# The last two chunks of an attention and feed-forward kernel: the product with w_out by seven block products in place of eight

## The chip, the cores and the metric

The kernel runs on one core of one Trainium2 chip. Five engines work beside each other, each with its own queue of instructions: TensorE (PE in the profile; its weight loads are PEld) multiplies matrices into PSUM, VectorE (DVE) and ScalarE (ACT) work elementwise, GpSimd (POOL) hardly computes here, and SyncE (SP) issues the DMA transfers. The metric is the device time of one execution in microseconds (us). Three executions of the kernel before took 653.5, 653.57 and 654.96 us; the median is 653.57.

## The reference

Eight batches of eight heads, 512 token rows and 32 state rows a head, 64 numbers a row. Tokens attend to the states and states to the tokens; the heads are put side by side, and a two-layer network follows, whose activation is h - tanh(h):

```
scores  = x @ state.T / 8;  a  = softmax(scores);   xread = a @ state
scores2 = state @ x.T / 8;  a2 = softmax(scores2);  sread = a2 @ x
y = concat([xread, sread], rows)       # (8 batches * 544 rows, 512)
h = y @ w_in                           # 512 -> 2048
out = (h - tanh(h)) @ w_out            # 2048 -> 512
```

All of it is float32. h - tanh(h) is an odd function: a row of y with its sign turned gives a row of the output with its sign turned.

## The kernel before

The rows are handled in nine **chunks**. Chunks 0 to 7 are the 512 token rows of a batch each; chunk 8 is the 256 state rows of all batches. For a token chunk the read of the states and w_in are folded into one matrix m (256 rows per half, made once per batch by `m_units` and `m_first_two` and kept in DRAM as `mdram`), so that the hidden layer of a token chunk is the product of the attention weights `aT` with m; that of chunk 8 is the state reads `srT` times w_in.

A chunk has 16 **steps**, one per block of 128 of the 2048 hidden columns. In a step, `hidden(f)` (lines 406 to 421) computes h for that block; `finish` takes tanh on ACT and the difference on DVE (line 426). Then `split` (lines 119 to 122) cuts the result into two parts: ACT rounds it to the faster matmul format (the high part), and DVE subtracts that from the original (the low part). Weights are cut the same way. A product of two such pairs takes three matmuls: high by high, high by low, low by high. `output(f)` (lines 431 to 460) multiplies the 128 hidden columns by 128 rows of w_out for each block of 128 tokens, three matmuls of 512 columns (lines 458 to 460), and adds up in PSUM over the 16 steps: four PSUM banks for a token chunk, two for chunk 8. After the last step the banks are copied to SBUF and stored.

Per step, a token chunk thus issues 6 hidden and 12 output matmuls of 512 columns; chunk 8 issues 12 hidden matmuls of 256 columns and 6 output matmuls of 512. Over a chunk of 512 tokens the product with w_out is 192 matmuls, over chunk 8 it is 96. `wo[f]` keeps both parts of w_out in SBUF, 16 tiles of 2 x 512 columns.

**Order.** The steps of all chunks stand in one list (line 849; 144 steps). In the loop (lines 851 to 894) the hidden step two places ahead (LAG = 2) is put before the output step, so hidden and output matmuls alternate on TensorE and a step's tanh, difference and cut have two steps' time. The other work (attention of later batches, the m of later batches) is hung on steps by the table `SCH` (line 163): a number in a list is the step at which one unit of that work is issued. Each unit is kept, on ACT and DVE, behind the tanh of its step (`issue_after`). Within these rules a planner orders the instructions of each queue by its own estimate of when each is ready; a matmul can so be put ahead of an earlier one whose operand it expects later. The first steps, up to step 8, follow an order written out by hand (lines 798 to 814).

**Loads.** SP issues every transfer. m of a chunk is loaded per quarter q (`load_m`, lines 229 to 250); batches 6 and 7 have their m in two addends, added on DVE (line 247). Chunk 8 loads w_in by quarters (`load_win`, lines 252 to 268). The state reads are turned for chunk 8 by eight PE transposes (`turn_sread`, lines 381 to 389).

## Time and profile before

| | |
|---|---|
| median of three runs | 653.57 us |
| the profiled execution | 653.85 us |
| its span, first to last instruction | 652.1 us |
| granted TensorE clock | 1.000 |
| PE busy | 646.6 us (99%), 3892 matmuls |
| DVE busy | 445.5 us (68%), 795 instructions |
| ACT busy | 355.6 us (55%), 645 instructions |
| POOL busy | 1.2 us, 7 instructions |
| DMA | 95.89 MB, all data on one queue (SP's) |

The span is 1.75 us shorter than the profiled execution's own time, which lies 0.28 us above the median. PE counts as busy while any matmul is in flight; since matmuls overlap, the busy share says that it never rests, and not how fast it goes: for that one reads the distance between the starts of two matmuls. In a row of the profile the operation stands as output <- inputs, with partitions x elements, count, total and mean time, and at the end the idle time of the engine before it and what ended it.

### The profile page before, as it was taken

The page shows a single profiled execution, that of the slowest core. Times are in us where ns is not written, and L with a number is a line of the kernel's source. Part 1 is how long each engine was busy: PE and PEld are TensorE (multiplying, and loading weights), DVE is VectorE, ACT ScalarE, POOL GpSimd, SP SyncE. Part 2 cuts the span into 40 slices and gives each one's busy share as a digit, 9 for nine tenths or more (in the row PEclk, how much of TensorE's full clock was granted, in tenths as well). Part 3 has the DMA queues.
Part 4 walks back from the last instruction along what each step waited for, and adds up shares of the span by engine and source line. Part 5 has one row for each costly group of instructions (what it writes and reads, how often), then busy time and mean ns, then how long its engine had stood idle before and what let it go on. Part 6 is the DMA issues. An engine that isn't in the chain of part 4 may idle for free.

```text
span 652.1 us, 10247 instructions
## 1 busy us (share of the span) xinstructions
PE 646.6 (99%) x3892; PEld 511.1 (78%) x3892; DVE 445.5 (68%) x795; ACT 355.6 (55%) x645; POOL 1.2 (0%) x7
## 2 busy tenths in 40 slices
PE   9999999999999999999999999999999999999997
PEld 6466766888877788887888788887887888888996
DVE  5998999898556676558765875458767654454442
ACT  4865668786665545546556655444534453333442
POOL 0000000000000000000000000000000000000000
PEclk9999999999999999999999999999999999999999
DMA  9994787267577512444366227353342202010310
GB/s 314 380 311 159 258 270 266 61 197 223 143 250 210 165 33 100 128 130 152 111 195 186 80 94 224 104 184 139 123 136 96 66 33 98 0 33 32 130 34 32
DMA packets 52209, 95.89 MB, mean 147 GB/s; under 512 B 6208, under 2 KB 21568, under 8 KB 52160
## 3 DMA queue, kind: packets, MB, share of 16 engines
q1 hardware_dynamic: 52160, 95.24, 45.3%
q8 instruction: 30, 0.49, 0.3%
q14 instruction: 19, 0.16, 0.1%
HBM read 64.29 MB, written 30.93 MB: 146 GB/s over the span
## 4 chain that ended last, share of the span: by engine, by line
PE 96%; DVE 1%; ACT 1%; DMA 0%; issue 0%; POOL 0%; ACTq 0%; POOLq 0%
PE ops L458 19%; PE ops L460 19%; PE ops L459 19%; PE hps L418 9%; PE hps L419 9%; PE hps L420 9%; PE hps L729 3%; PE mps L219 2%; PE mps L673 1%; PE rps L368 1%; PE ops L755 1%; PE pps L355 1%; PE mps L218 1%; PE sps L283 1%; PE warm L582 1%; PE hps L416 1%
## 5 line engine op out<-in xcount | busy, mean ns | idle before, releaser
L458 PE MATMUL ops<-wo,g 128*128 128x512 f32 x536 | 214.1, 401 | 0.1
L459 PE MATMUL ops<-wo,g 128*128 128x512 f32 x536 | 209.0, 390 | 0.0
L460 PE MATMUL ops<-wo,g 128*128 128x512 f32 x536 | 198.2, 391 | 0.0
L426 DVE TENSOR_TENSOR t<-hps,t 128x512 f32<-128x512 f32 (+1 forms) x134 | 87.7, 656 | 95.6 <-ACT t L426 94.8
L426 ACT ACTIVATE t<-hps 128x512 f32<-128x512 f32 (+1 forms) x134 | 76.3, 573 | 125.7 <-PE hps L420 124.3
L458 PEld LDWEIGHTS ops<-wo,g 128*128 128x128 f32 x536 | 100.6, 188 | 25.8 <-issue 2.5
L460 PEld LDWEIGHTS ops<-wo,g 128*128 128x128 f32 x536 | 100.2, 188 | 22.7 <-DVE g L122 0.8
L459 PEld LDWEIGHTS ops<-wo,g 128*128 128x128 f32 x536 | 100.7, 188 | 22.0 <-issue 2.2
L121 ACT CAST g<-t 128x512 fp32r<-128x512 f32 (+1 forms) x134 | 79.6, 596 | 61.7 <-DVE t L426 56.8
L122 DVE TENSOR_TENSOR g<-t,g 128x512 fp32r<-128x512 f32 (+1 forms) x134 | 87.4, 655 | 31.4 <-ACT g L121 29.6
L419 PE MATMUL hps<-aT,m 128*128 128x512 f32 x232 | 90.7, 391 | 0.0
L418 PE MATMUL hps<-aT,m 128*128 128x512 f32 x232 | 90.7, 392 | 0.0
L420 PE MATMUL hps<-aT,m 128*128 128x512 f32 x232 | 90.1, 391 | 0.0
L418 PEld LDWEIGHTS hps<-aT,m 128*128 128x128 f32 x232 | 43.5, 188 | 11.8 <-DVE t L426 1.3
L420 PEld LDWEIGHTS hps<-aT,m 128*128 128x128 f32 x232 | 43.6, 188 | 10.6 <-issue 1.7
L419 PEld LDWEIGHTS hps<-aT,m 128*128 128x128 f32 x232 | 43.6, 188 | 9.6 <-issue 0.8
L122 DVE TENSOR_TENSOR m<-mr,m 128x1024 fp32r<-128x1024 f32 x29 | 35.4, 1221 | 14.2 <-ACT m L121 13.7
L122 DVE TENSOR_TENSOR wst<-w,wst 64x512 fp32r<-64x512 f32 (+1 forms) x56 | 36.3, 648 | 6.1 <-ACT wst L121 4.5
L121 ACT CAST m<-mr 128x1024 fp32r<-128x1024 f32 x29 | 30.3, 1045 | 10.3 <-DMA mr<-md 10.2
L220 ACT COPY st<-mps 128x512 f32<-128x512 f32 (+1 forms) x56 | 30.2, 557 | 10.1 <-PE mps L219 9.1
L121 ACT CAST wst<-w 64x512 fp32r<-64x512 f32 (+1 forms) x56 | 32.9, 587 | 0.8
L481 DVE COPY ob<-ops 128x512 f32<-128x512 f32 x14 | 9.7, 690 | 16.4 <-DMA out_x<-ob 10.9
(219 smaller groups left out, 626.9 us busy)
## 6 DMA issues: line engine op xcount, KB each, us to landing
md<-st SPq DMA_DIRECT2D x96, 128.0 KB, 2.2
mr<-md SPq DMA_DIRECT2D x20, 512.0 KB, 3.7
xT<-in_xT SPq DMA_DIRECT2D x16, 512.0 KB, 5.5
xn<-in_xn SPq DMA_DIRECT2D x16, 512.0 KB, 4.2
out_x<-ob SPq DMA_DIRECT2D x32, 256.0 KB, 2.5
w<-wf SPq DMA_DIRECT2D x12, 512.0 KB, 4.3
wn<-wf SPq DMA_DIRECT2D x8, 512.0 KB, 4.0
ml<-md SPq DMA_DIRECT2D x6, 512.0 KB, 3.8
```

What stands on the lines that cost most here:

```text
L121: nc.scalar.copy(hi, src)
L122: return (sub or nc.vector).tensor_sub(lo, src, hi)
L219: nc.tensor.matmul(ps, s[:, 0, h], t[:, e], start=(g == 1), stop=True)
L220: nc.scalar.copy(stage[:, e], ps)
L418: nc.tensor.matmul(ps, mhi[k][:, cols], ahi[:, k], start=(k == 0), stop=False)
L419: nc.tensor.matmul(ps, mhi[k][:, cols], alo[:, k], start=False, stop=False)
L420: nc.tensor.matmul(ps, mlo[k][:, cols], ahi[:, k], start=False, stop=(k == nk - 1))
L426: tanhs.append((nc.scalar.activation(t, ps, AF.Tanh).ins, nc.vector.tensor_sub(t, ps, t).ins))
L458: nc.tensor.matmul(o, g[:, 0, tok], wo[f][:, 0], start=first, stop=False)
L459: nc.tensor.matmul(o, g[:, 0, tok], wo[f][:, 1], start=False, stop=False)
L460: return nc.tensor.matmul(o, g[:, 1, tok], wo[f][:, 0], start=False, stop=last).ins
L729: nc.tensor.matmul(hps[n], m[:, k], ats[b][k], start=(k == 0), stop=(k == 1))
```

## The change

For chunks 7 and 8 a new class `Seven` replaces `Chunk`. Each group of 256 tokens (two in chunk 7, one in chunk 8) is treated as a product of 2 x 2 blocks: the hidden values are blocks A of 128 tokens by 1024 hidden columns (even and odd blocks of 128), w_out is blocks B of 1024 by 256. Eight block products would be needed; Strassen's scheme in Winograd's form needs seven, with sums of blocks before and after:

```
S1 = A21+A22  S2 = S1-A11  S3 = A11-A21  S4 = A12-S2
P1 = A11 B11      P2 = A12 B21      P3 = S4 B22      P4 = A22 (B11-B12-B21+B22)
P5 = S1 (B12-B11) P6 = S2 (B22-B12+B11)  P7 = S3 (B22-B12)
```

The four results are sums of the seven. The parts of the change:

- **The products.** `finish` writes h - tanh(h) into a buffer `big` that holds all blocks; nothing is multiplied by w_out until the hidden steps are done. `operand` then cuts one block (128 x 1024) into high and low parts, three products ahead of its use (AHEAD = 3). `products` issues, for each of 8 depth steps, one matmul of the high part with 512 columns (the two parts of a 256-column weight block side by side) and one of the low part with 256; in P3 of chunk 8 three matmuls of 256. So a product is 16 matmuls, and a group of 256 tokens 112. `gather` adds the two halves of the bank and sums the products on ACT and DVE; `store` writes results of 128 x 256.
- **Sums of blocks of A.** S1 and S2 on DVE. S3 and S4 by accumulating DMAs from POOL's queue in chunk 7, by DVE in chunk 8. So that only additions are needed in chunk 7, half of batch 7's rows get their sign turned in the softmax sums (`signs`).
- **Sums of blocks of w_out** (`weight_sums`), in eight parts of three stages each, hung on steps 41 to 105 by the new list "sums": stage one puts the whole weights together again (two loads on SP, two accumulating DMAs on POOL's queue), stage two forms the four sums (three ACT instructions, four accumulating DMAs, of which three follow each other), stage three cuts them into parts (ACT 128 x 1024, DVE 128 x 1024) and stores both to DRAM (`tdram`). `fetch` loads a sum's parts for a product, eight transfers of 256 KB each on SP: those of P4 and P6 over a quarter of `wo`, those of P5 and P7 into tiles of their own.
- **Order.** In chunks 7 and 8 the loop of steps ends; hidden steps come first (even ones now in PSUM's `ps_o` banks), then the products in the order P4 P1 P5 P2 P6 P7 P3, for chunk 7 each for both groups. Loads and cuts of m and w_in for these chunks are issued earlier than before. m's second addend of batch 7 is added by an accumulating DMA and not by DVE. `SCH` has new numbers; the last attention unit of batch 7 moves from step 121 to 114.
- **Buffers.** Several tiles of earlier stages (raw w_in and w_out rows, kept scores, m of batch 1) now lie in slices of `big`.

The diff without the new numbers of `SCH` and the moves into `big`:

```diff
+AHEAD = 3
+FIRST = 7
...
+        return cut_m(b, q, raw_m(b, q))
+
+    def raw_m(b, q):
...
-            r = pool.tile([P, 2, 512], F32, tag="mr", name=f"mr{b}{q}", bufs=RRB)
+            tag, bufs = ("stage", SB) if b >= FIRST else ("mr", RRB)
+            r = pool.tile([P, 2, 512], F32, tag=tag, name=f"mr{b}{q}", bufs=bufs)
...
-            if len(addends) > 1:
+            if len(addends) > 1 and b >= FIRST:
+                nc.gpsimd.dma_start(r, addends[1].rearrange("g h n f -> (h n) g f"), accum_op=ALU.add)
+            elif len(addends) > 1:
                 r2 = pool.tile([P, 2, 512], F32, tag="stage", name=f"ml{b}{q}", bufs=SB)
...
+            if b < FIRST:
+                nc.vector.tensor_scalar_add(z, z, EPS)
+            else:
+                nc.vector.scalar_tensor_tensor(z, z, EPS, signs, ALU.add, ALU.mult)
...
+    blocks = big.rearrange("p f n -> p (f n)").rearrange("p (g r c k n) -> p g r c k n", g=2, r=2, c=2, n=P)
+
+    def weight_sums(p):
+        r = parts(f"wr{p}", [P, 2, 512], F32)
+        for c in range(2):
+            w = wo[2 * p + c].bitcast(F32)
+            nc.sync.dma_start(r[:, c], w[:, 0])
+            nc.gpsimd.dma_start(r[:, c], w[:, 1], accum_op=ALU.add)
+        yield
+        x = r.rearrange("p k (c n) -> p k c n", c=2)
+        t = parts(f"wt{p}", [P, 4, 256], F32)
+        nc.scalar.activation(t[:, 0::2], x[:, 0], AF.Copy, scale=-1.0)
+        nc.scalar.copy(t[:, 1], x[:, 0, 0])
+        nc.scalar.activation(t[:, 3], x[:, 1, 0], AF.Copy, scale=-1.0)
+        for to, add in ((t[:, 0], x[:, 0, 1]), (t[:, 2], x[:, 1, 1]), (t[:, 1], t[:, 2]), (t[:, 3], t[:, 1])):
+            nc.gpsimd.dma_start(to, add, accum_op=ALU.add)
+        yield
+        hi, lo = parts(f"wh{p}", [P, 4, 256], F32R), parts(f"wl{p}", [P, 4, 256], F32R)
+        split(hi, lo, t)
+        for c, part in enumerate((hi, lo)):
+            nc.sync.dma_start(tdram[:, :, p, 256 * c : 256 * c + 256], part.bitcast(F32))
+        yield
+
+    class Seven(Chunk):
+        ORDER = "P4 P1 P5 P2 P6 P7 P3".split()
+        banks = {}
+        seconds = []
+
+        def finish(self, f, ps):
+            n = self.n
+            t = blocks[:, : n // 256, :, f % 2, f // 2]
+            ps = ps.rearrange("p (g r n) -> p g r n", r=2, n=P)
+            nc.scalar.activation(t, ps, AF.Tanh)
+            Seven.gate = nc.vector.tensor_sub(t, ps, t).ins
+
+        def block(self, g, name):
+            return blocks[:, g, int(name[0]) - 1, int(name[1]) - 1]
+
+        def side(self, g, name):
+            a11, a12, a21, a22 = (self.block(g, x) for x in ("11", "12", "21", "22"))
+            out, a, b = {"S1": (a22, a21, a22), "S3": (a21, a11, a21), "S2": (a22, a22, a11), "S4": (a12, a12, a22)}[name]
+            if self.i == B:
+                (nc.vector.tensor_add if name == "S1" else nc.vector.tensor_sub)(out, a, b)
+            elif name in ("S1", "S2"):
+                nc.vector.tensor_add(out, a, b)
+            else:
+                nc.gpsimd.dma_start(out, b if out is a else a, accum_op=ALU.add)
+
+        HOME = {"P4": "22", "P1": "11", "P5": "22", "P2": "12", "P6": "22", "P7": "21", "P3": "12"}
+
+        def operand(self, x, g, ks):
+            if (x, g) not in self.parts:
+                self.parts[x, g] = (
+                    pool.tile([P, NFF // 2, P], F32R, tag="g", name=f"hi{self.i}{x}{g}", bufs=GB),
+                    parts(f"lo{self.i}{x}{g}", [P, NFF // 2, P], F32R),
+                )
+            hi, lo = self.parts[x, g]
+            with tc.issue_after(self.gate):
+                Seven.gate = split(hi[:, ks], lo[:, ks], self.block(g, self.HOME[x])[:, ks]).ins
+
+        def weights(self, x, k):
+            if x in ("P1", "P2", "P3"):
+                f, c = {"P1": (0, 0), "P2": (1, 0), "P3": (1, 1)}[x]
+                return wo[2 * k + f][:, :, 256 * c : 256 * c + 256]
+            if x in ("P4", "P6"):
+                return wo[2 * k][:, :, 256:512]
+            return Seven.seconds[k]
+
+        def fetch(self, x):
+            row = {"P5": 0, "P6": 1, "P7": 2, "P4": 3}[x]
+            if not Seven.seconds:
+                for k in range(4):
+                    tag, bufs = ("t", TB) if k < 3 else ("cr", CB)
+                    Seven.seconds.append(pool.tile([P, 2, 256], F32R, tag=tag, name=f"second{k}", bufs=bufs))
+                last = pool.tile([P, 4, 2, 256], F32R, tag="sm", name="second", bufs=1)
+                Seven.seconds.extend(last[:, k] for k in range(4))
+            for k in range(NFF // 2):
+                nc.sync.dma_start(
+                    self.weights(x, k).bitcast(F32), tdram[:, row, k].rearrange("p (c n) -> p c n", c=2)
+                )
+
+        def products(self, x, g, ks):
+            if (x, g) not in self.banks:
+                self.banks[x, g] = bank(ps_o, f"{x}{self.i}{g}")
+            o = self.banks[x, g]
+            hi, lo = self.parts[x, g]
+            last = NFF // 2 - 1
+            for k in ks:
+                w = self.weights(x, k)
+                if self.i == B and x == "P3":
+                    nc.tensor.matmul(o[:, :256], hi[:, k], w[:, 0], start=(k == 0), stop=False)
+                    nc.tensor.matmul(o[:, :256], hi[:, k], w[:, 1], start=False, stop=False)
+                    nc.tensor.matmul(o[:, :256], lo[:, k], w[:, 0], start=False, stop=(k == last))
+                    continue
+                both = lambda: nc.tensor.matmul(o.rearrange("p (c n) -> p c n", c=2), hi[:, k], w, start=(k == 0), stop=(k == last))
+                if k < last:
+                    both()
+                nc.tensor.matmul(o[:, :256], lo[:, k], w[:, 0], start=False, stop=False)
+                if k == last:
+                    both()
+
+        def gather(self, x, g):
+            o = self.banks.pop((x, g))
+            if g not in self.sums:
+                self.sums[g] = twins(f"c{self.i}{g}", [P, 4, 256], F32)
+            u = [self.sums[g][:, k] for k in range(4)]
+            if x == "P3" and self.i == B:
+                nc.vector.tensor_add(u[2], u[1], o[:, :256])
+                self.store(g, 0, 1, u[2])
+                return
+            p = u[{"P4": 3, "P1": 0, "P5": 1, "P2": 2, "P6": 0, "P7": 2, "P3": 2}[x]]
+            add, sub = nc.vector.tensor_add, nc.vector.tensor_sub
+            if self.i < B and x in ("P1", "P2", "P7", "P3"):
+                nc.scalar.activation(p, o[:, 256:], AF.Copy, scale=-1.0)
+                sub(p, p, o[:, :256])
+            else:
+                nc.scalar.copy(p, o[:, 256:])
+                add(p, p, o[:, :256])
+            if x == "P1":
+                sub(u[3], u[0], u[3])
+            elif x == "P5":
+                add(u[1], u[1], u[0])
+            elif x == "P2":
+                add(u[2], u[2], u[0])
+                self.store(g, 0, 0, u[2])
+            elif x == "P6":
+                add(u[1], u[1], u[0])
+                add(u[3], u[3], u[0])
+            elif x == "P7":
+                add(u[3], u[3], u[2])
+                self.store(g, 1, 0, u[3])
+                add(u[0], u[1], u[2])
+                self.store(g, 1, 1, u[0])
+            elif x == "P3":
+                add(u[2], u[1], u[2])
+                self.store(g, 0, 1, u[2])
+
+        def store(self, g, r, c, u):
+            t = 2 * g + r
+            nc.sync.dma_start((xout[self.i] if self.i < B else sout)[t * P : (t + 1) * P, 256 * c : 256 * c + 256], u)
+
+        def hidden_bank(self, f):
+            return ps_h if f % 2 else ps_o
+
+        def units(self, start=0):
+
+            i, gs = self.i, range(self.n // 256)
+            self.parts, self.sums, self.banks = {}, {}, {}
+            seq = [(x, g) for x in self.ORDER for g in gs]
+            each = 1.37 if i < B else 1.44
+            made = 2
+            for f in range(start, NFF):
+                if f == start:
+                    self.fetch("P4")
+                    self.fetch("P5")
+                self.hidden(f)
+                if f in (3, 7):
+                    self.cut(f // 4 + 2)
+                if f % 4 == 1 and f > 4:
+                    self.open(slice(f // 2 - 2, f // 2), seq[:made])
+                yield each
+            self.open(slice(6, 8), seq[:made])
+
+            def make(n):
+                if made <= n < len(seq):
+                    x, g = seq[n]
+                    self.operand(x, g, slice(0, 8))
+                    if x == "P5":
+                        self.side(g, "S2")
+                        self.side(g, "S3")
+                    elif x == "P2":
+                        self.side(g, "S4")
+
+            for n in range(made, AHEAD):
+                make(n)
+            for n, (x, g) in enumerate(seq):
+                for ks in ((range(6), range(6, 8)) if n == 0 else (range(8),)):
+                    self.products(x, g, ks)
+                make(n + AHEAD)
+                self.gather(x, g)
+                if g == gs[-1]:
+                    if x == "P4":
+                        self.fetch("P6")
+                    elif x == "P5":
+                        self.fetch("P7")
+                if i < B:
+                    if n == 2:
+                        chunks[i + 1].raw(0)
+                        if i + 1 < B:
+                            chunks[i + 1].raw(1)
+                    elif n in (5, 9):
+                        chunks[i + 1].cut(n // 9)
+                    elif n == 8 and i + 1 == B:
+                        with tc.issue_after(self.gate):
+                            turn_sread()
+                yield 2.77
+
+        raws = None
+
+        def raw(self, q):
+            self.raws = self.raws or {}
+            with tc.issue_after(self.gate):
+                self.raws[q] = raw_m(self.i, q) if self.i < B else raw_win(q)
+
+        def cut(self, q):
+            with tc.issue_after(self.gate):
+                self.m[q] = (cut_m if self.i < B else cut_win)(*((self.i,) if self.i < B else ()), q, self.raws[q])
+            q += 2 if self.i < B else 1
+            if q < 4:
+                self.raw(q)
+
+        def prepare(self, q):
+            pass
+
+        def open(self, ks, operands):
+            for x, g in operands:
+                self.operand(x, g, ks)
+                if x == "P4" and ks.stop == 8:
+                    self.side(g, "S1")
...
-    chunks = [Chunk(i) for i in range(B + 1)]
+    chunks = [(Chunk if i < FIRST else Seven)(i) for i in range(B + 1)]
...
+    sums = itertools.chain(*[weight_sums(p) for p in range(NFF // 2)])
+    end = HALF + NFF + HALF + NFF * (FIRST - 2)
+
+    def side_work(st):
+        advance(sums, SCH["sums"].count(st))
...
+    for st, (i, f) in list(enumerate(steps))[HALF:end]:
...
+        if st >= end - 7:
+            Seven.gate = tanhs[st][-1]
+            if st == end - 5:
+                chunks[FIRST].raw(0)
+                chunks[FIRST].raw(1)
+            elif st == end - 4:
+                chunks[FIRST].cut(0)
+            elif st == end - 2:
+                chunks[FIRST].cut(1)
...
+    st, passed = end, 0.0
+    for i in range(FIRST, B + 1):
+        for spent in chunks[i].units(LAG if i == FIRST else 0):
+            passed += spent
+            while passed > 3.79:
+                passed -= 3.79
+                with tc.issue_after(chunks[i].gate):
+                    side_work(st)
+                st += 1
```

More of the change, by code (lines that the diff above doesn't have):

```diff
@@ L204, in m_units @@
             for k in range(2):
-                w = pool.tile([P, 2, 512], F32, tag="wf", name=f"w1{g}{q}{k}", bufs=WB)[:, :, cols]
+                w = home(10 + 2 * (next(wfn) % 2), 2)[:, :, cols]
                 nc.sync.dma_start(w, wf[q][:, 2 * k : 2 * k + 2, cols])
@@ L250, in load_m, with raw_win, cut_win @@
         return [m[:, 0, k] for k in range(2)], [m[:, 1, k] for k in range(2)]
-    def load_win(q):
-        his, los = [], []
-        for k in range(2):
-            w = pool.tile([P, 2, 512], F32, tag="wf", name=f"wn{q}{k}", bufs=WB)
-            nc.sync.dma_start(w, wf[q][:, 2 * k : 2 * k + 2])
-            if k == 0:
-                m = pool.tile([P, 2, 2, 512], F32R, tag="m", name=f"wm{q}", bufs=MB)
-                split(m[:, 0], m[:, 1], w)
-                his += [m[:, 0, c] for c in range(2)]
-                los += [m[:, 1, c] for c in range(2)]
-            else:
-                for c in range(2):
-                    m = parts(f"wm{q}{c}", [P, 2, 512], F32R)
-                    split(m[:, 0], m[:, 1], w[:, c])
-                    his.append(m[:, 0])
-                    los.append(m[:, 1])
+    def raw_win(q):
+        raws = []
+        for k in range(2):
+            w = pool.tile([P, 2, 512], F32, tag="stage", name=f"wn{q}{k}", bufs=SB)
+            nc.sync.dma_start(w, wf[q][:, 2 * k : 2 * k + 2])
+            raws.append(w)
+        return raws
+    def cut_win(q, raws):
+        his, los = [], []
+        for k, w in enumerate(raws):
+            if k == 1 and q % 2:
+                halves = [pool.tile([P, 2, 512], F32R, tag="x", name=f"wm{q}{c}", bufs=XB) for c in range(2)]
+                for c in range(2):
+                    split(halves[c][:, 0], halves[c][:, 1], w[:, c])
+                    his.append(halves[c][:, 0])
+                    los.append(halves[c][:, 1])
+                continue
+            tag, bufs = ("aT", 1) if k else ("m", MB)
+            m = pool.tile([P, 2, 2, 512], F32R, tag=tag, name=f"wm{q}{k}", bufs=bufs)
+            split(m[:, 0], m[:, 1], w)
+            his += [m[:, 0, c] for c in range(2)]
+            los += [m[:, 1, c] for c in range(2)]
         return his, los
     def convert_wout(f, part):
-        w = pool.tile([P, 512], F32, tag="wor", name=f"wor{f}", bufs=RB)
+        w = big[:, 14 + f % 2]
         part.convert(w)
@@ L516, in convert_win @@
         if p % 2 == 0:
-            wfs[q, p // 2] = pool.tile([P, 2, 512], F32, tag=("wf", "stage")[q - 2], name=f"w0{q}{p // 2}", bufs=WB)
+            if q == 2:
+                wfs[q, p // 2] = home(10 + 2 * (next(wfn) % 2), 2)
+            else:
+                wfs[q, p // 2] = pool.tile([P, 2, 512], F32, tag="stage", name=f"w0{q}{p // 2}", bufs=SB)
         w0[q][p].convert(wfs[q, p // 2][:, p % 2])
@@ L625, in turn_back @@
         if j < 2:
[L626 removed]
+            ats[0][j] = big[:, 4 + j]
         else:
@@ L850, in attention_ffn @@
     steps += [(i, f) for i in range(2, B + 1) for f in range(NFF)]
-    for st, (i, f) in list(enumerate(steps))[HALF:]:
+    sums = itertools.chain(*[weight_sums(p) for p in range(NFF // 2)])
+    end = HALF + NFF + HALF + NFF * (FIRST - 2)
+    def side_work(st):
+        advance(sums, SCH["sums"].count(st))
+        advance(a0, SCH["a0"].count(st))
+        advance(second_split, SCH["at1"].count(st))
+        advance(first_split, SCH["at0"].count(st))
+        advance(late1, SCH["r1"].count(st))
+        for b in range(2, B):
+            n = SCH[f"att{b}"].count(st)
+            if n:
+                if b not in atts:
+                    atts[b] = new_attention(b)
+                advance(atts[b], n)
+        for g in range(2):
+            advance(m1[g], SCH[f"m{g}"].count(st))
+    for st, (i, f) in list(enumerate(steps))[HALF:end]:
         with ExitStack() as gates:
```

52 lines of the change are left out of this document (24 added, 28 removed).

## The prediction

> **What bounds the kernel now.** I read the page's busy times first, then its chain of waits, then busy time by stretch.
>
> ```profile
> span 652.1 us, 10247 instructions
> ...
> PE 646.6 (99%) x3892; PEld 511.1 (78%) x3892; DVE 445.5 (68%) x795; ACT 355.6 (55%) x645; POOL 1.2 (0%) x7
> ...
> PE 96%; DVE 1%; ACT 1%; DMA 0%; issue 0%; POOL 0%; ACTq 0%; POOLq 0%
> ```
>
> ```profile
> 200.00:330.00 130.00, 130.00 (x842) 105.12 (x841) 88.16 (x166) 70.74 (x125) 0.00 (x0) 1.00 0.42 130
> 330.00:470.00 140.00, 140.00 (x787) 113.49 (x789) 93.77 (x174) 75.28 (x132) 0.00 (x0) 1.00 0.46 144
> 537.00:608.00 71.00, 71.00 (x394) 59.42 (x393) 34.29 (x54) 26.30 (x45) 0.00 (x0) 1.00 0.15 52
> 608.00:652.00 44.00, 40.34 (x251) 36.02 (x249) 17.04 (x36) 16.26 (x38) 0.00 (x0) 0.99 0.15 50
> ```
>
> (A row: stretch, length, then PE, PEld, DVE, ACT, POOL busy, granted clock, DMA share, GB/s.) TensorE sets the time: never idle between 200 and 648 us, clock 1.00, 96% of the chain. DVE is busy 67% of the middle and 48% of the stretch in which chunks 7 and 8 run. So a matmul removed is time gained, as long as the other engines keep up. The price of a matmul is its distance to the next, not its 0.39 us duration. The timeline of TensorE in chunk 7 and in chunk 8:
>
> ```profile
> 569.79 0.39 PE L459 MATMUL ops<-wo,g 128*128 128x512 f32 x1
> ...
> 574.10 0.39 PE L460 MATMUL ops<-wo,g 128*128 128x512 f32 x1
> ...
> 608.80 0.28 PE L418 MATMUL hps<-srT,wm 128*128 128x256 f32 x1
> ...
> 610.24 0.40 PE L458 MATMUL ops<-wo,g 128*128 128x512 f32 x1
> ...
> 611.62 0.28 PE L418 MATMUL hps<-srT,wm 128*128 128x256 f32 x1
> ```
>
> Chunk 7: 20 rows, 4.31 us in 19 steps, 0.2268 us per 512-column matmul. Chunk 8: twelve 256-column matmuls in 1.44 us, 0.120 each; six of 512 columns in 1.38 us, 0.230 each. So the cost is 13.3 ns plus 0.417 ns per column, and weight loads of 0.19 us each don't slow even the short ones.
>
> **TensorE's share of the change.** Per 256 tokens the output product was 96 matmuls of 512 columns. Now it is 7 products of 8 steps, a step being one matmul of 512 columns (high part against both weight halves) and one of 256: 8 x (0.2268 + 0.120) = 2.774 us. Chunk 7 (two groups): 192 x 0.2268 = 43.55 becomes 14 x 2.774 = 38.84, saving 4.71. Chunk 8: 96 x 0.230 = 22.08 becomes 6 x 2.774 + 24 x 0.120 (its P3 has three short matmuls a step) = 19.52, saving 2.56. Should the long matmul cost 0.230 beside short ones, 0.5 us goes. The hidden products keep their counts. **TensorE: -7.3 us, bounds -6.8 and -7.3.**
>
> That counts columns, though the instructions rise from 96 to 112 per group. The Trainium skill ("TensorE: Matmul & The Clock Gate", Back-to-back issue gap) gives streams with weight loads about 81 ns at 128 columns and 131 ns at 512, nearly a fixed price per instruction. By it, 256 columns taken in between at an estimated 98 ns, 112 x 114.5 = 12.8 us would replace 96 x 131 = 12.6. The trace disagrees with 227 and 120 ns.
>
> **What the other engines must now deliver.** Hidden and output matmuls no longer alternate: 16 hidden steps, then the products, each of which needs an operand of 128 x 1024 cut in two by ACT and DVE, and sums. Durations by shape:
>
> ```profile
> L122 DVE TENSOR_TENSOR m<-mr,m 128x1024 fp32r<-128x1024 f32 x29 | 35.4, 1221 | 14.2 <-ACT m L121 13.7 <-DMA md<-st 0.2
> L121 ACT CAST m<-mr 128x1024 fp32r<-128x1024 f32 x29 | 30.3, 1045 | 10.3 <-DMA mr<-md 10.2
> L121 ACT CAST g<-t 128x512 fp32r<-128x512 f32 x118 | 73.1, 622 | 52.3 <-DVE t L426 47.4 <-PE ops L460 3.2 <-PE mps L673 0.9
> L426 DVE TENSOR_TENSOR t<-hps,t 128x512 f32<-128x512 f32 x118 | 80.9, 688 | 84.0 <-ACT t L426 83.3
> L426 ACT ACTIVATE t<-hps 128x512 f32<-128x512 f32 x118 | 70.2, 599 | 113.9 <-PE hps L420 112.5 <-PE hps L416 0.9
> L122 DVE TENSOR_TENSOR g<-t,g 128x256 fp32r<-128x256 f32 x16 | 6.8, 424 | 6.1 <-ACT g L121 5.2 <-PE ops L460 0.9
> L121 ACT CAST g<-t 128x256 fp32r<-128x256 f32 x16 | 6.5, 406 | 9.5 <-DVE t L426 9.4
> L426 ACT ACTIVATE t<-hps 128x256 f32<-128x256 f32 x16 | 6.1, 383 | 11.8 <-PE hps L420 11.8
> L122 DVE TENSOR_TENSOR g<-t,g 128x512 fp32r<-128x512 f32 x118 | 80.6, 687 | 25.2 <-ACT g L121 24.4
> L386 PE MATMUL tps<-ident,sr x8: 270/272/273, 596.8 to 597.5; 128*128 128x128 f32 x8
> ```
>
> Hidden stage, chunk 7: 6 x 0.2268 = 1.36 us a step against 0.60 of ACT and 0.69 of DVE; the m and first-operand cuts fit the remainder. Chunk 8: 1.44 against 0.38 and 0.42.
>
> DVE while chunk 7's products run: 12 whole operands at 1.22 (14.6), last slices of two (0.85), S1 and S2 twice (4.9), 30 sums of 256 columns at 0.42 (12.6), the next chunk's w_in cuts 3 x 1.22 + 2 x 0.69 (5.0), the turned state reads 2 x 0.69 (1.4), the last tanh difference 0.7: 40.1 us, of which some 2.9 (the last three products' sums) may come later, so 37.2 against TensorE's 38.8 + 0.9 of transposes. Chunk 8: 5 whole operands 6.1 + slices 0.85 + S1 to S4 4.9 + 14 sums 5.9 + 0.4 = 18.2 against 19.5. ACT has about 25 us in chunk 7. So DVE goes from half busy to about 93% and must not wait much.
>
> In strict program order that costs: after chunk 7's last hidden matmul 0.60 + 0.69 + 0.41 + 0.42 and four handoffs of 0.06 (an estimate; successors start 0.03 to 0.10 after) make 2.4 us plus some delay, the six ready steps cover 2.08: about 0.5 lost. P4's second group waits behind S1 (1.22) and its own slice: 1.0. In chunk 8 P1 waits the same way: 0.85; P2 and P6 behind S2, S3, S4: 0.35. Together 2.7. But TensorE's queue is written by a planner that moves ready matmuls ahead of late ones:
>
> ```profile
> 600.84 0.39 PE L458 MATMUL ops<-wo,g 128*128 128x512 f32 x1
> 601.07 0.39 PE L459 MATMUL ops<-wo,g 128*128 128x512 f32 x1
> 601.29 0.39 PE L458 MATMUL ops<-wo,g 128*128 128x512 f32 x1
> ...
> 601.98 0.84 PE L460 MATMUL ops<-wo,g 128*128 128x512 f32 x3
> ```
>
> Here the low-part matmuls (L460), whose operand was late, were held back without a gap. The six ready steps of the next product can fill such holes. Bounds 0 and 2.7; I take 1.4, the middle.
>
> **Weight sums, steps 41 to 105.** Eight times 0.62 + 2 x 0.41 + 1.05 us of ACT (19.9) and 1.22 of DVE (9.8, less three adds of m that go, 3 x 1.22: 6.1), over 64 steps or more than 260 us in which a third of DVE and 45% of ACT is free. They add 32 DMAs on SP's queue and 48 accumulating ones on POOL's, which the trace has none of. What waits for those: stage three's cast, which stops everything behind it on ACT, the next tanh above all, and so TensorE. Stage two's last three accumulations follow each other; stage three comes four steps (4 x 18 x 0.2268 = 16.3 us) later. Nearest rows:
>
> ```profile
> q1 hardware_dynamic: 52160, 95.24, 45.3%
> md<-st SPq DMA_DIRECT2D x96, 128.0 KB, 2.2
> mlast<-f SPq DMA_DIRECT2D x8, 128.0 KB, 5.5
> wn<-wf SPq DMA_DIRECT2D x8, 512.0 KB, 4.0
> wo5d<-in_wout SPq DMA_DIRECT2D x2, 512.0 KB, 10.6
> out_s<-ob SPq DMA_DIRECT2D x2, 128.0 KB, 1.8
> ```
>
> At 2.2 or 5.5 us each (idle and crowded queue), 1.4 + 3 x 5.5 = 17.9 at most, which the two hidden steps that TensorE is ahead cover. I take 0.3 us for crowding and the moved attention steps, bounds -0.2 (TensorE's idle there) and 3. S3, S4 and m's accumulations have over 10 us each. The sign on batch 7's 128x16 sums, and tiles moved into one buffer of the same depth, cost nothing.
>
> **Fetched weights.** Each of P4 to P7 is eight 256 KB pieces, 2.10 MB, on SP. A piece can go once the matmul that last read its place is done. The tight place is chunk 8: P6's pieces start 0.35 us into its P4, P7's follow, and P7's last is read 13.9 + 2.4 + 0.85 = 17.1 us after that start. They land by 2.4 (0.35 and 2.0 of latency, an estimate between 1.8 and 2.2) + 4.19 MB / rate. What a full queue moves, partly in 1 KB runs (w_in's columns):
>
> ```profile
> 10.00:14.00 4.00, 4.00 (x105) 2.71 (x102) 4.00 (x9) 2.98 (x7) 0.00 (x0) 1.00 1.05 396
> ...
> 34.00:38.00 4.00, 4.00 (x45) 2.58 (x45) 4.00 (x9) 2.41 (x6) 0.00 (x0) 1.00 1.06 288
> ```
>
> 288 to 396 GB/s: 13 to 17 us, just in time. Single transfers (512 KB in 4.0 us, 131 GB/s) are the far bound (34 us, 17 lost), but eight pieces overlap. I take 0. On SP the 16 issues at 0.4 us (0.81 for two, below) take 6.5 of chunk 8's 19.5 us; behind P7's waiting pieces stand only output stores, for which nobody waits soon. In chunk 7, P4's pieces wait for chunk 6's last steps; behind them may stand the m pieces of q = 2, needed 8 x 1.36 = 10.9 us later, and a load and an accumulation at the 4.0 us of the 512 KB row fit.
>
> **The end.**
>
> ```profile
> 647.96 0.39 PE L460 MATMUL ops<-wo,g 128*128 128x512 f32 x1
> 648.38 0.65 ACT L475 COPY ob<-ops 128x256 f32<-128x256 f32 x2 [0.77 <-PE ops L460]
> 648.78 0.81 SPq L476 DMA_DIRECT2D out_s<-ob  x2
> ```
>
> Now two copies (0.65) and two stores; after, one add (0.42) and one store of the same size: -0.2.
>
> **Sum:** -7.3 + 1.4 + 0.3 + 0 - 0.2 = -5.8. The span 652.1 becomes 646.3; the profiled execution took 653.85, 1.75 beside the span, and stands 0.28 above the median, so 646.3 + 1.75 - 0.28 = **647.8 us** (-0.9%).
>
> **The rivals.**
> *Everything is hidden:* no stall at all, 646.1. For it the planner's filling; against it DVE at 93%.
>
> *DVE becomes the bound (slower than before).* Place: the 21 products. 17 whole operands and 20 sums need ACT's half first. If DVE waits w for each, it is late by 37w less its slack, 2.5 + 1.3 us. The rows above show it waiting 25.2/118 = 0.21 us per g cut and 14.2/29 = 0.49 per m cut. At 0.21: 4.0 us, 650.4. From w = 0.30 all is eaten; at 0.49: 14.3 us, 660.7. Against it: those waits fell on a half-idle DVE; with a full queue and ACT below two thirds the halves are there early.
>
> *The fetch is slow.* If 4.19 MB come at 204 GB/s, P7 ends 5.8 us late and the time is unchanged, 653.6; below that it is slower. Every full stretch shown is faster. On that the Trainium skill ("DMA: Bandwidth & Descriptors", Latency and other measured facts) has a rule against the change: copies whose per-partition row pitch in HBM is a large power of two drop to 207 GB/s at 512 KiB. The new buffer's pitch is 64 KiB, below the pitches it lists; by its figure the estimate is 653.3. No run here shows it.
>
> *Accumulations block ACT.* Two hidden steps are 8.2 us, of which the chain from tanh to the low part takes 2.6, so 5.5 are left: they cost from 6.8 us each on (1.4 + 3 x 6.8 = 16.3 + 5.5), and each 0.24 us more costs 8 x 0.72 = 5.8, the whole gain. At 7.5 us: 664.6. Only 512 KB loads in the crowded start land that late.
>
> *Price per instruction,* as the page on TensorE has it: -7.3 becomes about +0.7, 655.8; the rows exclude it but for 1%.
>
> **Chances.** Forecast 60% (its own range 646.3 to 650.3), all hidden 5%, DVE 15% (a third of it still a gain, a third within the measure, a third slower), fetch 10% (7 no change, 3 slower), accumulations 9% (4 no change, 5 slower), per instruction 1% (slower). Within 0.3% is 651.6 to 655.5, about what can be told from no change. Faster 70%, same 16%, slower 14%. Range 645.5 to 654.5: all low bounds at once give 645.9, and what lies above is the slower cases and the last of those without a change.
>
> **What would show it.** TensorE's rows of the products at 0.227 and 0.120 apart, 2.77 us a product; 112 matmuls per group. Stalls: gaps before P4's last steps, P4's second group, chunk 8's P1. DVE over 90% busy in the products with few waits on ACT; more than 0.3 us a wait shows the second rival. Wrong would be gaps before chunk 8's P7 ended by a fetch, ACT casts of the weight sums ended by an accumulation, or TensorE idle before chunk 7.

## The result, and the profile after

The changed kernel takes 658.88 us (657.92 to 658.99, four runs) against 653.71 for the kernel before in the same runs: a ratio of 1.0072, interval 1.0059 to 1.0084. The forecast was 647.8. The profiled execution took 658.82 us. Lines of its page (busy time by engine, DMA queues, chain of waits), and three stretches (length, PE, PEld, DVE, ACT, POOL busy, granted clock, DMA share, GB/s): the middle as before, chunk 7's products, and the end:

```profile
span 657.0 us, 10827 instructions
...
PE 648.2 (99%) x3948; PEld 510.0 (78%) x3948; DVE 479.8 (73%) x849; ACT 380.5 (58%) x691; POOL 50.5 (8%) x65
...
q1 hardware_dynamic: 76128, 123.04, 57.6%
q0 software_dynamic: 8304, 12.06, 11.2%
...
PE 81%; DVE 10%; DMA 5%; ACT 2%; issue 2%; POOL 0%; SPq 0%; ACTq 0%; DVEq 0%; POOLq 0%
```

```profile
330.00:470.00 140.00, 140.00 (x819) 112.25 (x818) 95.58 (x171) 82.12 (x147) 20.86 (x24) 1.00 0.75 211
567.00:608.00 41.00, 40.69 (x228) 34.70 (x227) 34.34 (x52) 22.90 (x38) 3.51 (x4) 1.00 0.83 240
608.00:652.00 44.00, 44.00 (x315) 41.22 (x314) 33.39 (x62) 20.43 (x42) 0.00 (x0) 1.00 0.62 211
```

TensorE still fills 99% of the span, and by busy time nothing is amiss. But it is busy for 1.6 us longer with less to compute, and other engines have entered the chain. Setting the two timelines of TensorE against each other shows where. The last output matmul of chunk 6 and the last matmul of all, before:

```profile
538.16 0.39 PE L460 MATMUL ops<-wo,g 128*128 128x512 f32 x1
...
647.96 0.39 PE L460 MATMUL ops<-wo,g 128*128 128x512 f32 x1
```

and in the changed kernel:

```profile
548.57 0.39 PE L494 MATMUL ops<-wo,g 128*128 128x512 f32 x1
...
653.37 0.28 PE L613 MATMUL P<-wo,lo8P 128*128 128x256 f32 x1
```

At the end of chunk 6 the changed kernel is 10.4 us late (the expectations below take 9.5), at the end 5.4. The part that was to gain has gained 5.0 us. The loss lies in the 548 us ahead of it, where the forecast had 0.3 us.

Two things stand there in the changed kernel's timeline of TensorE (start, duration, what it waited for). First a stall, with its neighbours on ACT and SP:

```profile
476.06 0.89 SPq L519 DMA_DIRECT2D out_x<-ob  x2
...
479.45 0.39 PE L454 MATMUL hps<-aT,m 128*128 128x512 f32 x1
480.59 0.59 ACT L513 COPY ob<-ops 128x512 f32<-128x512 f32 x1 [4.03 <-DMA out_x<-ob]
481.07 1.14 ACT L129 CAST g<-t 128x512 fp32r<-128x512 f32 x2
481.75 0.62 PE L492 MATMUL ops<-wo,g 128*128 128x512 f32 x1 [1.91 <-ACT g L129]
482.17 0.63 PE L493 MATMUL ops<-wo,g 128*128 128x512 f32 x1
482.60 0.63 PE L492 MATMUL ops<-wo,g 128*128 128x512 f32 x1
...
485.15 1.20 PE L494 MATMUL ops<-wo,g 128*128 128x512 f32 x4
```

ACT copies an output tile and must wait 4.03 us until an earlier output store has left the buffer `ob`; the cast of g stands behind it on ACT, and TensorE loses 2.07 us: 2.30 lie between two starts that are 0.23 apart without a wait. Then its matmuls come 0.427 us apart until 485.4, at a granted clock of 0.50, which costs another 1.7 us. The Trainium skill ("TensorE: Matmul & The Clock Gate", Part 1) puts the array at half its clock, 426.7 ns per 512 columns, after an idle window of about 3.4 us; the spacing agrees, though 2.07 us of idle time were enough here. The other three runs of the changed kernel show a granted clock of 1.000 and take as long (657.9 to 659.0 us), so what they lose in place of these 1.7 us no trace shows. Smaller stalls (0.97, 0.47 and 0.46 us) stand at 96, 105 and 142 us, where the kernel before has none.

Second, and not to be seen in any stall: TensorE's rows in a stretch without a gap, before and after.

```profile
413.02 0.39 PE L458 MATMUL ops<-wo,g 128*128 128x512 f32 x1
...
437.72 0.39 PE L459 MATMUL ops<-wo,g 128*128 128x512 f32 x1
```

```profile
421.10 0.39 PE L492 MATMUL ops<-wo,g 128*128 128x512 f32 x1
...
442.43 0.39 PE L493 MATMUL ops<-wo,g 128*128 128x512 f32 x1
```

Before, 109 matmuls take 24.70 us, 0.2266 each. After, 92 take 21.33, 0.2318 each, at a granted clock of 1.00 and with the same durations of 0.39. In chunks 2 to 6 these 2.3% stand in the output steps 0 to 7 alone; in steps 8 to 15 the distance is 0.227 again. What both make adds up to nearly the whole: some 860 matmuls by 5.1 ns are 4.4 us, the large stall with the half speed behind it 3.8, the smaller ones 1.9, together 10.1 of the 10.4 us.

### The profile page after: what moved, and what is told of

The parts are those of the page before. It is cut to its first block, busy times and chain, and to the rows that moved or that the text cites. A ratio compares the mean times of both kernels' runs of the same rounds, so it can differ in the third digit from the quotient of the medians.

```text
span 657.0 us, 10827 instructions
## 1 busy us (share of the span) xinstructions
PE 648.2 (99%) x3948; PEld 510.0 (78%) x3948; DVE 479.8 (73%) x849; ACT 380.5 (58%) x691; POOL 50.5 (8%) x65
## 4 chain that ended last, share of the span: by engine, by line
PE 81%; DVE 10%; DMA 5%; ACT 2%; issue 2%; POOL 0%; SPq 0%; ACTq 0%; DVEq 0%; POOLq 0%
PE ops L492 14%; PE ops L493 14%; PE ops L494 13%; PE hps L452 7%; PE hps L453 7%; PE hps L454 7%; PE P L615 5%; PE hps L985 3%; PE P L618 3%; PE mps L231 2%; DMA out_x<-ob 1%; DVE big L554 1%; PE ops L1011 1%; PE rps L399 1%; PE pps L386 1%
## 5 line engine op out<-in xcount | busy, mean ns | idle before, releaser
L492 PE MATMUL ops<-wo,g 128*128 128x512 f32 x440 | 178.3, 407 | 1.9 <-ACT g L129 1.9
L493 PE MATMUL ops<-wo,g 128*128 128x512 f32 x440 | 173.7, 395 | 0.0
L494 PE MATMUL ops<-wo,g 128*128 128x512 f32 x440 | 163.0, 394 | 0.0
L460 DVE TENSOR_TENSOR t<-hps,t 128x512 f32<-128x512 f32 x102 | 70.1, 688 | 73.1 <-ACT t L460 72.6
L460 ACT ACTIVATE t<-hps 128x512 f32<-128x512 f32 x102 | 60.7, 598 | 92.1 <-PE hps L454 89.2
L492 PEld LDWEIGHTS ops<-wo,g 128*128 128x128 f32 x440 | 83.0, 189 | 25.9 <-issue 3.6
L493 PEld LDWEIGHTS ops<-wo,g 128*128 128x128 f32 x440 | 83.1, 189 | 20.7 <-issue 3.0
L494 PEld LDWEIGHTS ops<-wo,g 128*128 128x128 f32 x440 | 82.4, 188 | 20.1 <-DVE big L159 0.8
L130 DVE TENSOR_TENSOR g<-t,g 128x512 fp32r<-128x512 f32 x102 | 69.6, 687 | 23.7 <-ACT g L129 22.0
L129 ACT CAST g<-t 128x512 fp32r<-128x512 f32 x102 | 63.0, 622 | 29.2 <-DVE t L460 26.1
L130 DVE TENSOR_TENSOR m<-mr,m 128x1024 fp32r<-128x1024 f32 x27 | 33.0, 1221 | 9.7 <-ACT m L129 9.4
L130 DVE TENSOR_TENSOR wst<-big,wst 64x512 fp32r<-64x512 f32 (+1 forms) x56 | 36.3, 648 | 4.2 <-ACT wst L129 2.4
L129 ACT CAST wst<-big 64x512 fp32r<-64x512 f32 (+1 forms) x56 | 32.9, 588 | 0.7
L528 POOL DMA_DIRECT2D wr<-wo x16 | 14.2, 1007 | 236.9 <-DVE big L159 104.5
```

The lines of the kernel that those rows point to most:

```text
L129: nc.scalar.copy(hi, src)
L130: return (sub or nc.vector).tensor_sub(lo, src, hi)
L460: tanhs.append((nc.scalar.activation(t, ps, AF.Tanh).ins, nc.vector.tensor_sub(t, ps, t).ins))
L492: nc.tensor.matmul(o, g[:, 0, tok], wo[f][:, 0], start=first, stop=False)
L493: nc.tensor.matmul(o, g[:, 0, tok], wo[f][:, 1], start=False, stop=False)
L494: return nc.tensor.matmul(o, g[:, 1, tok], wo[f][:, 0], start=False, stop=last).ins
```

## The experiments

Every kernel was run beside the kernel before (653.5 to 653.8 us); times are medians, with the ratio and its interval.

**Is it the weight sums?** The first theory was that their transfers crowd the queues, the rival that their work on ACT and DVE delays the tanh chain. e1 leaves the sums out of the changed kernel, so its last products are not those of the reference. e2 keeps the changed kernel's step numbers and buffers, but the old product. e3 adds the sums to that, unused; e4 adds only transfers, of the same number and sizes.

```
e1: "sums": []  ;  fetch reads wf in place of tdram
e2: FIRST = 9, "sums": []
e3: FIRST = 9
e4: FIRST = 9, weight_sums without activation, copy and split
```

> The changed kernel without the weight sums (none of their stages is issued; the fetches read other numbers of the same size and layout from the stored w_in, so the products of the last two chunks are not those of the reference). Theory A (the sums' transfers crowd the DMA queues, loads and stores land late, ACT and DVE wait for them in order): the 7 us that the changed kernel loses between the start of the sums and the end of chunk 6 come back, 651 to 653 us. Theory B (the sums' work on ACT and DVE): the same. Theory C (the new step numbers and the shared buffer): the loss stays, 657 us or more.

> The changed kernel's step numbers and buffers, with the old product with w_out for all chunks and without weight sums. A and B: only the 2 us that are lost before the sums begin, 655 to 656 us. C: the whole loss of 9.5 us, about 662 us.

> As the one with the old product and the new step numbers, and the weight sums are made and stored, though nothing reads them. A and B: 7 us more than without the sums, about 662 us. C: no more than without them.

> As the last, but of the weight sums only the transfers are left, as many and as large as before, with the same order among themselves; the three ACT instructions and the cut on ACT and DVE are left out (what is stored is not the sums; nothing reads it). A: nearly all of the sums' cost stays, 661 us. B: it goes, 656 us.

e1 took 660.68 us (1.0103, 1.0079 to 1.0126), e2 663.41 (1.0148, 1.0133 to 1.0163), e3 664.93 (1.0164, 1.0146 to 1.0182). Both theories of the sums fell: the changed kernel is no faster without them, and beside the old product (e3 against e2) they add 1.5 us, with intervals that overlap. The third theory of these expectations, numbers and buffers, holds: a kernel with neither sums nor new product is 9.9 us slower than before. e4 came to 697.22 us (1.0667), and its waits between 140 and 235 us (total, times, longest) say how:

```profile
ACT st L232 <- DMA md<-st: 23.9, 7, 7.4
```

The transfers run unspaced there (e4 issues its 48 accumulations between 107 and 249 us, the changed kernel all but two between 239 and 508), the stores of the state rows leave late, and ACT, which must write the next rows into their buffer, stops with everything behind it. Here the transfers were made denser than the change makes them, so e4 gives no share of its loss.

**Step numbers or buffers?** e6 is the changed kernel with the old step numbers and the sums; e7 the same with the old product and no sums, so that only the buffers and the loading differ from before; e8 the kernel before with nothing but the new numbers; e9 is e2 with the attention of batches 5 to 7 at its old numbers.

```
e6: SCH of before, with "sums" of after
e7: FIRST = 9, SCH of before, "sums": []
e8: the kernel before, SCH of after
e9: FIRST = 9, "sums": [], "att5" to "att7" of before
```

> The changed kernel, complete with its sums and seven products, with the step numbers of the kernel before for attention, m and w_out (the list of the sums stays). Theory C1 (the new numbers bunch side work on a few steps, and that alone makes the loss before chunk 7): the loss of 9.5 us falls to the 1.5 that the sums cost, about 651 us, faster than before. Theory C2 (the shared buffer and the other moves of tiles make it): no change, about 659 us.

> Old product, no weight sums, the step numbers of before, but the new buffers and the new loading of w_in for chunk 8. C1: like the kernel before, 653 to 655 us. C2: about 663 us as with the new numbers.

> The kernel before with nothing changed but the step numbers, which are those of the changed kernel. C1: about 663 us. C2: about 654 us.

> Old product, no weight sums, new buffers, the new step numbers except for the attention of batches 5, 6 and 7, which stand at their steps of before. If the bunched attention of batch 6 (five units at step 90, three at 94) makes the 4 us that are lost between 460 and 500 us: 659 us, and no stall of TensorE over 1 us there. If not: 663 us.

e6: 660.04 us (1.0091, 1.0076 to 1.0106). e7: 658.51 (1.0076, 1.0059 to 1.0092). e8: 663.81 (1.0152, 1.0131 to 1.0173). e9: 661.32 (1.0111, 1.0096 to 1.0126). Each of the two costs time alone, e8's numbers 10 us and e7's buffers 5; together, in e2, they cost 9.9, so they don't add up. The traces show why: the same numbers stall TensorE more in e8 (6.9 us over seven stalls, and 1.6 at half speed) than in e2 (5.3 us over five, none at half speed). e8 has the stall at 480 us in the old kernel:

```profile
477.16 0.40 PE L420 MATMUL hps<-aT,m 128*128 128x512 f32 x1
480.07 0.79 PE L458 MATMUL ops<-wo,g 128*128 128x512 f32 x1 [2.52 <-ACT g L121]
```

In e9 it is gone: the new numbers put five of batch 6's nine units into step 90. But e7 shows no idle time of TensorE over 0.12 us between 85 and 640 us, and was 5 us slower all the same. What it has is 0.230 us a matmul on the mean between 200 and 440 us, against 0.227 in the kernel before and in e8.

**Where tiles lie.** The slow output steps are those that read `wo` 0 to 7, which lie near the start of SBUF, ahead of the working pool. The steps that read `wo` 8 to 15, in the working pool with the tiles `g`, are fast. In the kernel before, all wide tiles start at 128 within 256 bytes of a partition. The change's tile `signs`, 64 bytes, moved the working pool to 192 and left `wo` 0 to 7. (These places are the addresses in the built programs; the traces don't show them.) e10 puts an unused tile of 64 bytes into the kernel before; e11 makes `signs` 128 bytes. With the latter go two variants: e12 with the old numbers for batches 5 and 6, e13 with all old numbers but batch 7's attention and with sums that start earlier and leave out batch 6's steps.

```
e10: + pad = cpool.tile([P, 16, 1], F32, name="pad")
e11: signs = cpool.tile([P, 32, 1], ...)[:, :16]
e12: e11, "att5" and "att6" of before
e13: e11, SCH of before, "att7" of after, "sums": [30, 34, 38, 38, ..., 82, 86, 86, 98, 102]
```

> The kernel before with nothing changed but one unused tile of 64 bytes per partition put behind sr (written once at the start, never read). It moves every tile of the working pool by 64 bytes, while w_out's first eight tiles (wo 0 to 7) stay. Theory P (placement to 128 bytes): before, all wide tiles start at multiples of 128 bytes; in the changed kernel the 64-byte tile of signs put the working pool 64 bytes off, and the matmuls of the output steps 0 to 7 of each chunk, which read wo 0 to 7 against the tiles g, come 0.232 us apart in place of 0.227. Then this kernel shows the same slow stretches, half of each of chunks 2 to 7 and of chunk 1, some 1000 matmuls by 5 ns: about 5 us, 657.5 to 660 us. Theory D (distance or bank: the 32 KB tile big pushed the working pool away from wo): 64 bytes do nothing, 653.5 to 654.5 us and 0.227 us throughout.

> The changed kernel with its tile of signs made 128 bytes long (the second half unused), so that the tiles behind it start at multiples of 128 bytes again. Theory P: the slow stretches go, about 5 us less than the changed kernel's 658.9, so 652.5 to 655 us, and the matmuls of output steps 0 to 7 are 0.227 us apart; the stalls at 96 us and 479 us stay, since they come from the step numbers. Theory D: nothing changes, 658 to 659.5 us, 0.232 us in these stretches.

> The same with the attention of batches 5 and 6 at the step numbers of the kernel before (five of batch 6's nine units stood in one step in the changed kernel). If both causes hold, the stall of 2 us at 480 us and the half-speed matmuls behind it go as well, some 3 us: 649.5 to 652 us. If placement is not a cause: 655 to 657 us. If the sums' work at these steps stalls TensorE as well (as where the old numbers were kept with the sums, 1.3 and 1.4 us), only about 1 us is gained by the numbers: 652 to 654 us with placement.

> The same with all step numbers of the kernel before but two: batch 7's attention keeps the changed kernel's numbers (its end at step 114 lies ahead of the seven products), and the weight sums start at step 30 in place of 41 and leave out steps 87 to 97, where batch 6's attention stands. If placement, early numbers and the crowding of attention with sums are the whole loss, what is left is the shorter last part (5 us gained) less the sums' work: 648 to 650.5 us, faster than both kernels. If the sums cost their time wherever they stand (1.5 us): 650 to 652 us. If placement is not a cause: 654 to 657 us.

e10: 658.95 us (1.0082, 1.0064 to 1.01), for 64 bytes that nothing reads. e11: 655.86 (1.0035, 1.002 to 1.0051), yet its slow stretches stood (93 matmuls 0.2312 us apart), so the rule of 128 bytes had fallen. Of its 3 us less, 1.3 are in the span of the profiled execution, where the stall at 480 us is milder (0.90 and 1.11 us, no half speed after it); the rest the traces don't show. e12: 656.77 (1.0046, 1.0029 to 1.0064); the stall moved to DVE's cut of g (1.38 us): with the sums in the same steps the attention's numbers alone don't help. e13: 654.19 (1.0008, 0.9996 to 1.0019), slow stretches still there. With 128 bytes the pool lies at 0 and `wo` at 128, so the next guess was 256.

```
e14: signs = cpool.tile([P, 64, 1], ...)[:, :16]
e15: pad of 32 elements (128 bytes)     e16: pad of 64 (256 bytes)
e17: e13 with the signs of e14
```

> The changed kernel with its tile of signs made 256 bytes long, the rest of it unused. In the kernel before, wo 0 to 7 and the whole working pool start at the same place within 256 bytes (at 128); with 64 bytes of signs the pool starts at 192, with 128 bytes at 0, and both kernels are slow in output steps 0 to 7 of each chunk; with 256 bytes it is at 128 again. Theory P256 (wo and g must lie alike within 256 bytes): 0.227 us a matmul throughout, about 5 us less than with 128 bytes of signs, 650 to 652.5 us. Theory P512 or coarser (within 512 bytes or more): still 0.230 us on the mean, 655 to 659 us.

> The kernel before with an unused tile of 128 bytes behind sr: its working pool starts at 0 within 256 bytes, wo 0 to 7 at 128. Theory P256: slow in output steps 0 to 7, as with 64 bytes, 657.5 to 660 us. If only a shift by 64 bytes matters: 653.5 to 654.5 us.

> The kernel before with an unused tile of 256 bytes behind sr: its working pool starts at 128 within 256 bytes, as wo 0 to 7 do. Theory P256: no change, 653 to 655 us and 0.227 us a matmul. Theory P512, or any move of the pool against wo 0 to 7: slow, 657.5 to 660 us.

> The kernel with all step numbers of before but batch 7's attention, the sums from step 30 and none of them in steps 87 to 97 (654.2 us with 128 bytes of signs), now with 256 bytes of signs. Theory P256: the slow stretches were what was left, some 5 us: 648.5 to 651 us, faster than the kernel before. Theory P512: 653.5 to 655 us.

e15: 657.53 us (1.0059, 1.0046 to 1.0072). e16: 653.41 (0.9997, 0.9988 to 1.0006). e14: 654.82 (1.0015, 1.0005 to 1.0024). e17: 651.71 (0.9975, 0.996 to 0.999). The same stretch of TensorE in e10, e15, e16 and e14, first and last row:

```profile
415.83 0.40 PE L460 MATMUL ops<-wo,g 128*128 128x512 f32 x1
...
441.32 0.39 PE L462 MATMUL ops<-wo,g 128*128 128x512 f32 x1
```

```profile
414.50 0.39 PE L460 MATMUL ops<-wo,g 128*128 128x512 f32 x1
...
439.73 0.39 PE L461 MATMUL ops<-wo,g 128*128 128x512 f32 x1
```

```profile
413.41 0.39 PE L460 MATMUL ops<-wo,g 128*128 128x512 f32 x1
...
438.34 0.39 PE L462 MATMUL ops<-wo,g 128*128 128x512 f32 x1
```

```profile
417.99 0.39 PE L492 MATMUL ops<-wo,g 128*128 128x512 f32 x1
...
438.85 0.39 PE L493 MATMUL ops<-wo,g 128*128 128x512 f32 x1
```

With 64 unused bytes 110 matmuls are 0.2317 us apart, with 128 bytes 109 are 0.2315 apart, with 256 bytes 110 are 0.2266 apart, and in the changed kernel with 256 bytes 92 are 0.2267 apart. In e10, seven chunks of eight steps with 18 matmuls each, by 5.1 ns, make 5.1 us; measured were 5.2. That the places of `wo` and `g` relative to each other within 256 bytes decide over the distance is shown for the three tried: the pool's own place doesn't, since steps 8 to 15, with both tiles in it, are fast wherever it lies. Why it is so is not shown. Nor does it explain everything: chunk 8's 512-column matmuls in the kernel before and the seven products stand 0.230 to 0.234 us apart at any of these placements. And the times of the changed kernel follow less closely than its rows: from 128 to 256 bytes of signs the profiled executions go from 657.42 to 653.37 us, the medians only from 655.86 to 654.82, above the 650 to 652.5 expected; e13 and e17, with the old numbers, are 2.5 us apart. e14's single runs reach from 653.1 to 655.9. Its stalls seem to come out differently each time; that is argued, since each kernel has one trace.

**What is left.** e17 stands still for 1.21 us at 296 us, for attention inputs (`xT`) that land too late. e18 moves the sums off such steps; e19 is e18 without them, so its last products are not those of the reference, and it has no such stall.

```
e18: "sums": [28, 32, 36, 36, 40, 44, 44, 48, 52, 52, 57, 62, ..., 79, 83, 86, 86, 98, 102]
e19: "sums": []  ;  fetch reads wf in place of tdram
```

> The kernel with 256 bytes of signs and the old step numbers (651.7 us), with the sums moved off the steps in which an attention's inputs are asked for or first used (38, 54, 56, 61, 69, 73): there TensorE stood still for 0.45 us at 216 us and 1.21 us at 295 us, waiting for inputs that queued behind the sums' transfers. If the queue was the cause, both stalls go: 649.5 to 650.5 us. If the sums' transfers cost the same wherever they stand, the stalls turn up elsewhere: 651 to 652.5 us.

> The same kernel without the weight sums; the transfers that fetch the sums read other memory of the same size and layout instead, so four of the seven products are made from wrong weights (the amount of work on TensorE and of the fetch is kept). If well-placed sums cost nothing, the time is that of the run with the sums, within 0.7 us; if their work costs time wherever it stands, this kernel is 1 to 2 us faster, 648 to 649 us.

e18 became slower, 656.81 us (1.0038, 1.0026 to 1.0051); e19 took 648.82 (0.9922, 0.9908 to 0.9936). The rows of ACT and TensorE around e18's largest stall:

```profile
193.17 0.86 POOL L536 DMA_DIRECT2D wt<-wt  x1 [6.18 <-DMA wt<-wt]
...
196.62 1.05 ACT L129 CAST m<-mr 128x1024 fp32r<-128x1024 f32 x1 [6.06 <-DMA mr<-md]
...
199.82 1.04 ACT L129 CAST wh<-wt 128x1024 fp32r<-128x1024 f32 x1 [2.15 <-DMA wt<-wt]
200.77 0.58 ACT L232 COPY st<-mps 128x512 f32<-128x512 f32 x1
...
201.40 0.50 PE L230 MATMUL mps<-wst,sms 128*128 128x512 f32 x1 [2.97 <-ACT st L232]
```

ACT waits first for a load that stands among the stores, then for an accumulation of the sums; TensorE loses 3.1 us, and runs at half speed until 205 us. So the sums' price depends on where each unit meets another wait: 3.5 us in e17, 8 in e18. With the new step numbers it can't be told, for there e1, without the sums, is the slower one by 1.8 us.

## Why the prediction was wrong

The four parts of the result, as differences of ratios, by 653.6 us: the products, with old numbers and 256-byte placement and no sums (e19), -0.78%, -5.1 us. The sums at the better places (e17 against e19), +0.53%, +3.5. The new step numbers, the sums' own among them (e14 against e17), +0.40%, +2.6. The 64 bytes (the changed kernel against e14), +0.57%, +3.7. Their sum is +4.7, the measured 1.0072. The parts are prices in this surrounding: the new numbers, 2.6 us here, cost 10 in the old kernel (e8), where the stalls come out longer.

- *"The sign on batch 7's 128x16 sums, and tiles moved into one buffer of the same depth, cost nothing."* **This step failed**, and not by a wait: 64 bytes of signs made some 860 matmuls of chunks 1 to 6 (six chunks, eight steps of 18) slower by 5.1 ns, 4.4 us by the rows and 3.7 by the times. The times are the weaker measure: e11, whose matmuls are still slow, lies only 1.0 us above e14, so most of the 3.7 came with the step from 64 to 128 bytes, for which only the milder stall is seen. In the kernel before, where nothing else moves, the price is plain: 5.2 and 4.0 us for 64 and 128 bytes, none for 256. The sum counted matmuls at one fixed price, and the change had altered the price.
- *"0.3 us for crowding and the moved attention steps", with bounds of -0.2 and 3.* **Failed as well:** 6.1 us, the sums 3.5 and the numbers 2.6. The free third of DVE and 45% of ACT were means over 260 us; batch 6's attention stands in steps 90 to 96, and the extra transfers lengthened `out_x<-ob` from 2.5 to 3.6 us and `md<-st` from 2.2 to 3.2. That ACT would wait there for an output store was in none of the rivals.
- *TensorE -7.3 us, stalls in the products +1.4.* The mechanism was right. e19 gains 5.1 us and the last part of the changed kernel 5.0, where 5.9 were forecast. Mis-sized was the product:

```profile
590.64 0.40 PE L618 MATMUL P<-wo,lo7P 128*128 128x256 f32 x2
...
604.76 0.40 PE L618 MATMUL P<-second,lo7P 128*128 128x256 f32 x2
```

  Five products take 14.12 us, 2.82 each in place of 2.774: the 512-column matmul costs about 0.234 us beside short ones, which over 20 products is 1.0 us, more than the 0.5 allowed. In e17, with the better placement, a product takes 2.82 as well. The stalls were some 1.3 us; the largest stood before P4's second group:

```profile
579.96 0.39 PE L618 MATMUL P<-wo,lo7P 128*128 128x256 f32 x1 [0.31 <-DVE lo7P L130]
```

- *DVE as the bound.* It didn't come: 34.34 of 41 us busy among chunk 7's products, 84% where 93% were forecast, and the 0.31 us above is the longest wait of a product for it.
- *Slow fetch.* No wait of a product for its weights in the changed kernel (one of 0.49 us in e19, which fetches from other memory). `second<-tdram`, 256 KB, landed in 5.8 us (median).
- *Accumulations block ACT.* Not in the changed kernel, but in e18, where the units came closer to other waits: 2.15 us of an ACT cast, as that rival had it, after a longer wait for a load.
- *Price per instruction.* Excluded: 112 matmuls in place of 96 per group, and the last part is shorter.
- *What would show it wrong:* "TensorE idle before chunk 7" was named, and it is there. But of the 10.4 us only 4.0 are idle time; the rest no gap shows.

The range, 645.5 to 654.5, missed: it left out the slower cases, which had 14%. And those that were named, a busy DVE, a slow fetch, blocking accumulations, a price per instruction, are not what came: a higher price of the old matmuls, and attention and sums that meet in-order waits on ACT.

e17 is the fastest kernel here that does the whole change, 651.71 us, 1.9 below the kernel before. Its single runs reach from 649.5 to 655.9.

## What to carry to other kernels

Before pricing a change by counting matmuls, compare their start-to-start distance in gapless stretches of both profiles; where it differs at a full clock, look at where the operands lie, and let an added tile be a multiple of 256 bytes long. Work that is free on the mean has to be placed against the stretches where it isn't, and each in-order wait on ACT (for a store buffer, for an accumulation) is a place where all of it meets.

## What the runs showed that had not been expected

- Matmuls with `wo` and `g` at different places within 256 bytes (128 against 192, or 128 against 0) come 0.2315 to 0.2318 us apart, at equal places (128 and 128) 0.2266, at a granted clock of 1.00 in both. The hidden matmuls in between are part of these stretches; in e10 the output matmuls alone come 0.233 us apart.
- After 2.07 us lost to a wait in the changed kernel, 2.7 us in e8 and 3.1 us in e18 TensorE ran at 0.427 us a matmul for 3.4 us, at a granted clock of 0.50; after 2.8 us in e2 it did not.
- Accumulating transfers of 128 KB landed in 3.0 to 3.2 us where they were spaced as in the change, and in 5.6 us in e4.
